# Shifted copies of V through DRAM: one write and four reads in place of sixteen SBUF copies

## The chip, the cores and the metric

One core of a Trainium2 chip. The metric is the device time of one execution in microseconds (us), the median of several runs. Ratios are the mean time of one kernel's fast runs over that of the other's in the same rounds, so not quite the ratio of the medians quoted beside them.

## The reference, cut to what matters

Four layers, A B A B, on x of 2048 positions by 512 features, with a residual and a layer norm around each. The change touches layer B, an attention over the 8 positions 0, 2, ... 14 back:

```python
W, dil = 8, 2                                  # 32 heads of 16 features
idx = pos[:, None] - (jnp.arange(W) * dil)[None, :]
kg = k[:, :, idx_c, :]                         # B, H, S, W, Dh
vg = v[:, :, idx_c, :]
logits = where(mask, einsum("bhsd,bhswd->bhsw", q, kg) * scale, -1e9)
o = einsum("bhsw,bhswd->bhsd", softmax(logits), vg)
```

## The kernel before

The 2048 positions are worked on in four blocks of 512. For each block the weights of the window lie with partition = 32 x (shift group) + head, and the product with V needs V in the same layout. So for each of four features `dl` there must be a row for every (shift, head): the same row of V, moved by 2 positions from one group of 32 partitions to the next. The kernel before makes these rows with four SBUF-to-SBUF DMAs per feature, sixteen a block, all on the one queue of SyncE (SP):

```python
def vrep(dl):
    if dl % 2 == 0:
        self.Vg[L, b][dl // 2] = self.big([2, NB * KVW], "Vg")
    for g in (0, 2, 1, 3):                     # KVW = 528, VGW = 2104 elements
        a = T["V"][dl:dl + 1, 0:1, 2 + 2 * g:3 + 2 * g]
        src = bass.AP(a.tensor, a.offset, [[4 * a.ap[0][0], H], [1, VGW]])   # 32 rows
        nc.sync.dma_start(out=self.Vg[L, b][dl // 2][32 * g:32 * g + 32, dl % 2, 0:VGW], in_=src)
# its consumer, on VectorE, once per feature q (4096 products per partition)
nc.vector.tensor_tensor(out=pv, in0=PT..., in1=<windows of Vg[q // 2][:, q % 2]>, op=ALU.mult)
```

The nine transposes of the normalised x (`xnT<-xn`) feed the projections. In layer A a small factor is already sent through DRAM and read back with broadcast (`Prho<-rd`), from a source of 8 x 16 rows:

```python
src = bass.AP(a.tensor, a.offset, [[2 * 16 * P, 8], [0, 16], [1, 16 * P]])
nc.sync.dma_start(out=pr[:].rearrange("p t a i -> p (t a i)"), in_=src)       # Prho<-rd
...
nc.sync.dma_start_transpose(out=self.xnT[...], in_=self.xn[...])              # xnT<-xn
```

The sequence of all steps (`_ORDER`), the buffer that each tile takes (`_SLOTS`) and the engine of each step that could run on two (`_CHOICE`) are fixed strings that a search has found. They give each engine its instructions in one fixed order.

## Time and profile before

| | |
|---|---|
| time | 333.1 us (332.5 to 334.3) |
| span of the profiled run | 329.5 us |
| busy: PE, VectorE (DVE), ScalarE (ACT) | 95%, 92%, 85% |
| VectorE's wait for the V copies | 1.2 us in all |
| DMA engines in the two B layers (93.7 to 173 and 247.8 to 313 us) | 80% and 92% busy, at 138 and 150 GB/s |

A busy share is time with an instruction under way, over the span. A wait line reads: who, waiting for whom: us in all, how often, the longest. The lines themselves are in the prediction.

### The profile page before, as it was taken

To read this page: it belongs to the slowest core of one execution; us is meant where nothing else is said; L and a number is where in the kernel's file an instruction comes from. 1 tells how busy PE (TensorE), PEld (TensorE's weight loads), DVE (VectorE), ACT (ScalarE), POOL (GpSimd) and SP (SyncE) were. 2 spreads that over 40 slices of the span, in tenths; PEclk is the share of its full clock that TensorE was granted. 3 is DMA by queue.
4 is the path that set the end of the run, shared out by engine and by line. 5 is a ranking of instruction groups with operands and counts; after the bars stand their busy time and mean duration, and the time that the engine had idled before them with its cause. 6 is when DMAs were issued, how large, how long until landed. Compare 5 with 4: busy or idle time off the path is not lost.

```text
span 329.5 us, 8061 instructions
## 1 busy us (share of the span) xinstructions
PE 311.5 (95%) x3203; PEld 149.7 (45%) x3203; DVE 302.7 (92%) x443; ACT 279.2 (85%) x634; POOL 26.9 (8%) x50
## 2 busy tenths in 40 slices
PE   8999999999999999899999999789999999997892
PEld 3645456435444454344443464543554444442330
DVE  8999994988999999899999999699999999999992
ACT  4999997999988979799999999699997887766550
POOL 4000000000040004000000000000004042400000
PEclk9999999999999999999999999999999999999998
DMA  7990000013757699994670300023359969799733
GB/s 200 313 252 6 0 2 4 2 47 92 127 141 152 143 156 138 139 157 98 114 148 4 64 3 2 4 69 90 116 72 190 133 130 147 138 150 160 161 115 120
DMA packets 37389, 35.42 MB, mean 107 GB/s; under 512 B 23008, under 2 KB 32224, under 8 KB 37344
## 3 DMA queue, kind: packets, MB, share of 16 engines
q1 hardware_dynamic: 36816, 34.81, 54.4%
q8 instruction: 27, 0.44, 0.7%
q14 instruction: 18, 0.15, 0.2%
q10 hardware_dynamic: 528, 0.02, 0.1%
HBM read 10.50 MB, written 2.36 MB: 39 GB/s over the span
## 4 chain that ended last, share of the span: by engine, by line
PE 60%; ACT 13%; DMA 12%; DVE 7%; SPq 3%; issue 2%; ACTq 0%; DVEq 0%
PE ps L893 18%; PE ps L516 9%; DMA Vg<-V 7%; PE ps L601 6%; PE ps L589 6%; PE ps L694 5%; DMA xnT<-xn 4%; PE ps L981 3%; ACT Ek L595 3%; ACT Eq L702 3%; PE ps L1045 2%; SPq L945 2%; DVE Eq L812 2%; PE ps L456 2%; ACT sqd L536 2%
## 5 line engine op out<-in xcount | busy, mean ns | idle before, releaser
L893 PE MATMUL ps<-xnT,WB 128*128 128x512 bf16 x384 | 88.4, 380 | 0.8 <-DMA xnT<-xn 0.8
L1036 DVE TENSOR_TENSOR pav<-PT,Vg 128x4096 bf16<-128x4096 bf16 (+1 forms) x34 | 71.8, 2162 | 1.9 <-DMA Vg<-V 1.2
L974 DVE TENSOR_TENSOR prod<-QT,K 128x4096 bf16<-128x4096 bf16 x32 | 72.2, 2285 | 0.5 <-ACT K L189 0.3
L893 PEld LDWEIGHTS <-WB 128*128 128x128 bf16 x384 | 42.3, 114 | 44.1 <-issue 7.6
L516 PEld LDWEIGHTS <-oT 128*128 128x128 bf16 x256 | 23.6, 98 | 33.6 <-ACT oT L189 4.3
L189 ACT CAST oT<-ps 128x512 bf16<-128x512 f32 (+1 forms) x55 | 29.5, 584 | 8.1 <-PE ps L1045 7.7
L702 ACT ACTIVATE Eq<-ps 128x512 bf16<-128x512 f32 x64 | 34.6, 617 | 1.3 <-PE ps L694 1.3
L595 ACT ACTIVATE Ek<-ps 128x512 bf16<-128x512 f32 x64 | 33.8, 612 | 0.8 <-PE ps L589 0.8
L516 PE MATMUL ps<-WoB,oT 128*128 128x512 bf16 x128 | 32.8, 380 | 0.3 <-ACT oT L189 0.2
L516 PE MATMUL ps<-WoA,oT 128*128 128x512 bf16 x128 | 30.9, 380 | 0.8 <-DVE oT L187 0.8
L694 PE MATMUL ps<-xnT,WA 128*128 128x512 bf16 x128 | 31.3, 380 | 0.2 <-DVE Eq L812 0.2
L536 ACT ACTIVATE sqd<-x 128x512 bf16<-128x512 bf16 x48 | 29.9, 629 | 1.3 <-DVE x L529 1.1
L601 PE MATMUL ps<-WA,xnT 128*128 128x512 bf16 x128 | 30.6, 379 | 0.0
L589 PE MATMUL ps<-WA,xnT 128*128 128x512 bf16 x128 | 30.4, 379 | 0.0
L529 DVE SCALAR_TENSOR_TENSOR x<-ps,x 128x512 bf16<-128x512 f32 x38 | 24.9, 684 | 1.4 <-PE ps L516 1.3
L189 ACT CAST K<-ps 128x512 bf16<-128x512 f32 x32 | 18.7, 591 | 3.6 <-PE ps L893 3.3
L189 ACT CAST QT<-ps 128x512 bf16<-128x512 f32 x31 | 18.2, 600 | 3.0 <-PE ps L893 3.0
L1045 PE MATMUL ps<-pav,indAV 128*32 128x512 bf16 (+1 forms) x272 | 17.5, 370 | 3.3 <-DVE pav L1036 2.9
L935 POOL COPY vh<-V 128x64 bf16<-128x64 bf16 x6 | 7.5, 1244 | 161.7 <-ACT V L189 161.7
L526 ACT ACTIVATE x<-ps 128x512 bf16<-128x512 f32 x26 | 15.1, 593 | 6.2 <-PE ps L519 5.7
L601 PEld LDWEIGHTS <-xnT 128*128 128x128 bf16 x128 | 12.3, 98 | 14.7 <-issue 0.4
L589 PEld LDWEIGHTS <-xnT 128*128 128x128 bf16 x128 | 12.3, 98 | 14.6 <-ACT xnT L189 0.4
(127 smaller groups left out, 451.1 us busy)
## 6 DMA issues: line engine op xcount, KB each, us to landing
Vg<-V SPq DMA_DIRECT2D x128, 131.5 KB, 4.5
Prho<-rd SPq DMA_DIRECT2D x8, 512.0 KB
x<-in_A_x_dram SPq DMA_DIRECT2D x3, 512.0 KB, 7.2
WB<-in_B_wqkv_dram SPq DMA_DIRECT2D x3, 512.0 KB, 8.9
wraw<-in_A_wqkv_dram SPq DMA_DIRECT2D x4, 256.0 KB, 4.5
out_dram<-x SPq DMA_DIRECT2D x4, 256.0 KB, 2.2
out_dram<-x SPq DMA_DIRECT2D x8, 128.0 KB, 2.5
x<-in_A_x_dram SPq DMA_DIRECT2D x4, 128.0 KB
```

What stands on the lines that cost most here:

```text
L189: self.nc.scalar.copy(out=out, in_=in_)
L516: nc.tensor.matmul(y[:], lhsT=oT[:, c, t * P:(t + 1) * P], rhs=Wo()[:, c, :], start=(c == 0), stop=(c == NB - 1 and not onpe))
L529: nc.vector.scalar_tensor_tensor(out=xb[:, t, :], in0=T[t][:], scalar=1.0, in1=xb[:, t, :], op0=ALU.mult, op1=ALU.add, **kw)
L536: nc.scalar.activation(out=sqd[:], in_=xb[:, t, :], func=ACT.Square, accum_out=T["ss"][:, t:t + 1])
L589: nc.tensor.matmul(pk[:], lhsT=xnT[:, t, k, :], rhs=self.WA[:, k, D:2 * D], start=(k == 0), stop=(k == NB - 1))
L595: nc.scalar.activation(out=T["E"][:, t, s, :], in_=T["k", t][:], func=ACT.Exp, scale=1.0 - 2.0 * s)
L601: nc.tensor.matmul(pv[:], lhsT=xnT[:, t, k, :], rhs=self.WA[:, k, 2 * D:3 * D], start=(k == 0), stop=(k == NB - 1))
L694: nc.tensor.matmul(pq[:], lhsT=self.WA[:, k, hb * P:(hb + 1) * P], rhs=xnT[:, :, k, :], start=(k == 0), stop=(k == NB - 1))
L702: nc.scalar.activation(out=self.Eq[L, b][s][:, :, hb, :], in_=T[hb][:].rearrange("p (t i) -> p t i", t=4), func=ACT.Exp, scale=1.0 - 2.0 * s)
L893: nc.tensor.matmul(pp[:], lhsT=self.WB[:, k, i * D + c:(i + 1) * D:NB], rhs=xnT[:, :, k, :], start=(k == 0), stop=(k == NB - 1))
L974: nc.vector.tensor_tensor(out=pr[:], in0=QT[:, c:c + 1, :].to_broadcast([P, NW, TB]), in1=win, op=ALU.mult)
L1036: nc.vector.tensor_tensor(out=pv, in0=PT[:, :, lo:lo + n].unsqueeze(1).to_broadcast([P, NB, 2, n]), in1=vw, op=ALU.mult)
```

## The change

Its intent: to move V out of SBUF once and to let one DMA per feature fetch all four shifted copies, five DMAs a block instead of sixteen. A new search made new strings for order, slots and choices. The diff, cut to its core (the strings and two options that are switched off are left out):

```diff
+    "v_dram": ((0, 0), (0, 1), (0, 2), (0, 3), (1, 0), (1, 1), (1, 2), (1, 3)),
...
+        def vwr():
+            self.VD[L, b] = self.dram.tile([P, NB * KVW], BF16, name="vd%d%d" % (L, b))
+            nc.sync.dma_start(out=self.VD[L, b][:], in_=T["V"][:].rearrange("p c t -> p (c t)"))
+
         def vrep(dl):
...
+            if (L, b) in _OPT["v_dram"]:
+                a = self.VD[L, b][dl:dl + 1, 2:3]
+                src = bass.AP(a.tensor, a.offset, [[2, 4], [4 * NB * KVW, H], [1, VGW]])
+                nc.sync.dma_start(out=self.Vg[L, b][dl // 2][:, dl % 2, 0:VGW], in_=src)
+                return
...
+        if (L, b) in _OPT["v_dram"]:
+            add(st + "v", "SP", vwr)
```

More of the change, by code (lines that the diff above doesn't have):

```diff
@@ L44 @@
     "split": ((1, 2), (1, 3)),
+    "v_dram": ((0, 0), (0, 1), (0, 2), (0, 3), (1, 0), (1, 1), (1, 2), (1, 3)),
+    "half_mo": (),
+    "rho_pad": 0,
     "warm": 14,
@@ L54 @@
 _ORDER = """
-9 d6 b6 8 e a c 0 0 d i i i 0 0 i i i f h i i i i i i i i g j k o p j l 3 1x 1y t 3 1x t u m b o q r 34 1z s t
-x 2 2 1q 1r 1x 1x 1x n 1q 21 20 1x v w w 1s 1q 22 23 1q 1q 1t 1u 1q 4i 1w y 3d 3d 3d 3e 1v 3e 4 z 6 3e z 25 z
-z 10 1h 3e z 11 25 25 25 15 13 1h 1h 5 12 12 12 16 12 26 1h 26 26 26 26 1i 3e 1 28 28 26 14 18 26 26 d5 2g 2g
-bh 2j 17 2g 18 3e 2g 18 18 19 2a 1h 1n 1j 1o 2h 2h 2h 2h 2h 2h 2h 18 1f 1a 1c 2h 1k 3d 3e 3e 1b 1b 1l 1k 1e 2k
-1k 1k 1p 1b 1b 2d 1m 2j 2j 2m 2d 7 2l 32 32 33 1d 33 2d 2d 2e 3d 2r 7 2r 1g 28 2o 2o 2d 33 2i 29 2o 2o 33 3a
@@ L60 @@
-28 2s 2s 2c 2p 3a 3a 2r 3a 35 35 35 2s 2s 2s 2s 2r 2s 32 27 2s 2j 2o 32 2b 3b 37 38 33 33 33 33 2u 2u 2u 2z 2z
-2u 3a 2z 2z 3e 30 3a 3a 2f 2f 2f 2f 2q 2q 2v 2q 2n 2q 3f 2y 35 3f 3a 3a 2z 2t 31 bs 2w 31 2x 3b 36 31 39 31 3c
-3g 3a 3c 3g 3g 3c 3c 3m 3f 3n 3o 3o 3o 3g 3g 3g 3f 3p 3q 3g 3g 3f 3r 5l 3q 24 24 24 3h 3g 3p 3t 3v 3i 3i 3u 5m
-5n 3s 3q 3q 3q 3q 3h 3i 5m 7 3p 3w 3y 3h 3h 24 24 3x 3q 3z 3q 3q 3q 3i 5l 3i 3i 3i 3i 3h 5p 5o 5m 5m 3j 5q 5m
-5r 3i 3k 5l 5s 5t 5v 5m 3k 3j 3k 5u 3k 5m 5m 7g 7h 7i 40 43 41 44 7h 42 5m 3j 3j 5m 24 7 45 3k 3k 3k 3k 24 46
@@ L65 @@
-45 47 5w 5z 5y 5x 48 60 45 49 47 45 4a 47 47 61 61 62 4b 3j 47 4b 4f 94 4c 4d 7j 61 3k 45 45 4e 45 4g 45 64 7j
-7j 4h 65 61 66 95 63 63 63 63 4k 4u 4u 67 4k 4k 4u 4v 96 63 95 97 4l 67 6a 6b 4j 4w 4m 7h 4x 7h 4p 4q 7k 7l 4k
-7n 68 4n 4p 4r 69 97 3l 6c 7m 7o 7p 50 4p 4s 50 7q 4p 7p 4t 7s 7r 7r 7p 7t 7r 7p 97 7u 4u 4y 4o 7r 4z 6j 6k 6o
-6p av 6o 6q 6o 6o 50 6t 7v 7r 6e 95 7v 6e 7y 7z 7w 95 6f 7x 6s 6r 6g 6v 6j 6l 98 99 9c 9a 6e 6v 6e 6i 4j 6d 9b
-6j 6m 9d 9d 9e 6h 6v 6j 9d 9d 9g 9f 6u 6w 6w 6w 6n 80 8c 3l 82 9f 9h 9f 9i 9f 8h 6v 6w 9j 8d 51 9f 6u 6u 6x 50
@@ L70 @@
-87 6d 6x 6w 9j 83 87 9k 6u 88 51 8j 51 51 9m 9l 6x 6v 6y 9n 9o 89 82 84 82 4z 4z 52 52 8c 8e 8c 8c 4z 85 8f 87
-87 8b 8a 8g a0 50 51 a1 a0 a0 81 52 6z 6y 6z a3 71 70 6y 6y 6z 72 6z 73 9q a2 81 9p 9r 74 75 76 8i 74 50 77 74
-78 76 76 9v 9w 74 79 76 9v 9v 53 9y 53 53 53 54 54 54 54 55 56 8i 7a 57 58 8j 82 76 7a 7d 7e 59 7c 59 8i 59 59
-7b 86 5a 5c 5b 8j 8j 5e 5b 5d 5b 5b 9x 5f 5b 7f a5 a7 5f 5j 5h 5i 9q 9s 9q 9t 5g 9q 8k 8k 8k 8k 9v a7 8l a7 8l
-a0 9u a4 8k 8l 8i c3 c3 c4 c4 c4 9z 8j b4 b5 b5 c4 c3 c4 c4 c3 c4 c4 b7 b7 b4 b5 5k b8 a8 a8 a7 a8 a8 a9 a9 b5
@@ L75 @@
-8m 8m b9 c1 8m c2 c2 a6 a6 at au a8 a9 b4 aw at at au au au au aw 8n ax 8n 8p 8n 8m 8n b5 c3 8r 8o a6 ay a7 c1
-c2 a6 au c2 8q 8s 8s 8v 8t c4 8u aa aa 8s 8s 8u 8w 8x aa 8u 8u 8y aa c1 c2 aw aw b0 8u 8y 91 b5 at 92 8z b4 b5
-b5 ab c2 ac az ab ab ae ab 90 93 ad bc bc bc bc b7 b7 af ag ah ag ag ag aj ak bb al au c1 bi au bi bf bf bf b1
-bd ai ai ai ai bi bj am ai b1 am b1 b1 aq ao an ba ar bc bg bg bg bg bg bg ag ag bf ag bl ag ap bq b2 as bq bq
-bq bg b1 bg br br br br br br b3 b3 b3 b3 be be be be c2 by by by by c2 c1 bz br br bn by bn bn c2 bt bu c5 c6
@@ L80 @@
-c6 c5 bt bn bo c5 by by by by bv c5 bn bt bi bm c6 c6 c6 c6 c6 c6 bt bk bp bp bp bz by bp c0 c0 bw bx c0 c0 c9
-c5 ca c6 cb cb cb cc cd fr ce cd c7 c8 c8 cc ch cf fs ft cg ci cc cj cm cd cl cd e2 fs e3 c7 e4 cd c7 c7 c8 c8
-c8 cd cd ck cd e3 c8 c8 c8 cd cd e2 e5 e7 c7 c8 e6 e3 e3 e3 cn co cp hb e8 cq cr hc e2 eb ea e9 fu fu ec cs ct
-e3 cu e3 e3 e3 cs cv e3 cs fs hd hc ed ee eg cs ef cw eh ei ei ei ei cx ej cu cu cu fu cy fs fv cu cy cz em d0
-d2 d3 fw fz el fx cs cs he cs cs fy g0 g0 g0 g1 d1 d4 en ek g3 ek ek ek eo ek g2 g2 g4 g2 he he dc dc eo er g0
@@ L85 @@
-g5 g2 hc dh de dh g6 g2 dj g6 g9 ga g7 di g8 d7 d7 dd d8 d7 d7 d9 hc hf hg ep hh dh dh es hj db eq dl hi dc dc
-dn dn dk d6 hk hk gb hk et ev da dm ev df f0 hl hm dg fa ew dn hn dn hm dm ho ex f1 ev ey hm fc f0 hk f2 fc hp
-hm hq do do do do f0 f0 dp dp dn f3 dm dm fc f4 do dp dn hm hq gd hr f5 f5 f5 f5 ev ht hu dq dq dq hs hv gi f7
-f6 eu f9 gi gk f8 gi fb dr dq dr dt gl ez fc gi eu gc gd gm fd gf fd fd ge gj i2 i3 dr dr fd gd gd fe fe fd fb
-gn dv gn gg fb fb gn gn gs gu gu gu fe fc go gh gp i7 i7 ds i8 i9 gv gq gv gr gt gu gv gv gw hx gw gv gw i7 ia
@@ L90 @@
-hy i7 ff fg fh ff fg gu fi ff i2 ib i4 i2 i2 hx hx i5 hx hz i6 i0 du dw dx gt ic ie if ie ie i1 dw dy gc hw id
-id id id if fg if ie if ig ig ff dw e0 fj if ig dw e1 gx gt gy fg gz fk fl fl fl fn fm fo fp fl fq ie ih ii ih
-ih ih ih ii ii ij ik gt il io ii im io gx gx gx io ii in ip iq ip is ir ip it io ir ip gy h0 gy gx h1 h4 ir gy
-dz iu ir iv dz h4 h2 h5 h5 h6 iw h8 gy iv h4 h3 h5 h4 h5 h7 h7 h9 fo ha h7 h7
+34 0 0 0 27 d5 8 i i i i i i i i i i i i i i 9 0 a d 3 4i f g c 1x h e j k 3 1x o p j l m b t t 1y av o 2 2 1q
@@ new lines @@
+1z 1x 1x u q 1r t v 21 w n 1q x r w 20 1x 1x bh 23 2i 22 1s s 1q 1q 1q 1q 1w y 3d 3e 4 3d z z z z 1u 7 7 3d 3d
+1v 1t bs 25 3e 5 18 18 18 3e 3e 10 18 z 13 15 3e 11 25 3e 1 3e 3e 19 28 16 28 28 26 28 26 29 2a 12 12 12 18 1a
+25 1e 25 1b 1c 26 26 2c 26 26 1f 2b 26 6 26 14 2g 2h 2h 1h 1h 1h 1b 1h 1d 1i 12 2g 2h 2h 1b 1b 1g 17 2j 1h 1j
+1o 2j 2l 2k 2g 2h 2h 1k 1l 1k 1n 1k 1k 2g 2r 2h 2h 2d 2d 1m 32 7 7 2d 2d 2o 2s 2s 2o 2e 2o 2o 33 33 2d 2u 24
+32 33 33 3a 2u 2w 2r 2s 1p 2s 2r 2t 2r 2s 2j 2p 3a 3a 2j 2s 2s 2s 32 2m 32 35 33 33 2o 3a 33 33 3b 2z 2z 2z 3f
@@ new lines @@
+3g 3g 2f 2f 2n 2f 2z 2f 2q 2q 36 3a 30 3d 3a 3a 3a 2u 2u 2x 2y 3f 2z 35 35 35 2q 3a 24 24 24 24 24 2q 37 2v 31
+31 3e 38 31 3g 3b 3a 31 3c 3c 3c 39 3c 3m 3f 3l 3n 3o 3o 3o 3f 3p 3q 3g 3g 3g 3g 3g 5l 3f 3h 3r 3q 3g 3p 5m 3v
+3u 3s 3i 3t 3i 3q 3q 3h 3p 3y 3w 5n 3q 3q 3h 3h 24 3z 3i 3i 3i 3i 5m 3i 3q 3x 3q 3q 3j 3k 5l 5o 5p 3i 3q 3h 3k
+3i 7g 5m 5m 5q 5m 5r 40 44 43 3j 7h 41 7i 5l 5u 5m 5s 5m 5t 7h 7j 7j 7j 3j 3k 3j 42 45 45 5v 5m 3k 3k 3k 3k 3k
+5m 5m 5w 5y 46 48 5z 45 45 5x 47 60 47 49 47 4a 47 4b 47 61 61 64 4b 4c 3j 4d 3k 94 4f 61 4g 45 45 62 45 45 4h
@@ new lines @@
+4e 61 63 63 95 96 65 4k 66 63 63 95 97 97 4u 4l 4v 67 63 4j 4p 4q 4p 4p 4p 7h 67 6a 4s 4u 68 69 6b 6c 7h 7k 7l
+7m 4r 97 7n 4k 4k 7o 4n 7p 7p 4t 4w 50 7q 4u 4u 7p 7s 4m 7p 50 b6 7t 7r 7u 6j 6j 4y 6e 6e 4x 4z 50 4z 4z 7r 7r
+7r 6k 4k 6l 7v 7r 6o 6o 6f 6e 95 95 7v 7z 7y 6g 4o 6p 7w 7x 6t 6h 4j 6q 98 9c 99 50 6v 6o 6o 6e 9a 9b 9d 6s 9d
+6j 6j 9e 9g 6r 9d 9d 6i 80 82 9f 9f 6n 51 51 6m 9h 6v 6v 9f 9i 9f 83 6d 6d 6v 51 51 52 52 9j 9f 6w 6w 6w 6w 6x
+6u 6u 50 87 6x 51 9j 9l 9m 6w 87 6x 9k 89 87 8c 8a 88 8c 9n 8e 87 6u 8h 8b 8j 6u 8c 6u 3l 6v 6y 6y 6y 6y 52 82
@@ new lines @@
+82 50 85 82 86 6z 6z 8f 71 70 9o 8c 8g 9q 9q 4z 4z 8d 6z 6z 9r 72 9s a0 73 74 a1 74 84 75 76 77 76 53 a0 53 a2
+74 81 81 74 a5 78 76 79 9q 9t 76 9v 9w 54 54 55 53 53 8i 8i 54 54 57 8i 8i 8i a0 a0 7a 76 56 a7 7a 58 59 a3 7b
+7e a4 9p a6 7d 59 5c 5a 5b 59 7c 8j 8j 5b 59 5e 8j 5d 5b 9v 9v 5b 9v 5f 9z 9x a7 9y 5b 5f 8k 5j 8k 8k 8k 8l 8l
+7f c3 c4 c4 5g c3 c3 c4 c4 c4 c4 5i b4 b5 9q 9u a6 a6 5h a7 a7 8k 8l 5k 8j b4 b4 b4 a8 a8 a8 a8 b5 b5 b5 b5 b5
+b5 a6 a9 a9 c1 c1 c1 a8 b7 a6 b7 c1 8m 8m c2 8m 8m c2 c2 c2 c2 b5 at at b8 b9 c2 c2 8n 8n 8n a9 8o a7 8n 8p au
@@ new lines @@
+au at 8r au 8q 8s au 8s 8t aa aa au au bc aa 8s 8v 8s 8w 8u 8x 8u 8u 8u aw ax at au b7 aw ba aw 8y 8u ay ab ab
+ac ad ab aa ab af 8y 91 c3 ae ag 90 au 8z 92 bc b7 ag c4 bc bc c4 bd bb b1 ag ah aj ak c2 ai ag ai al ai b1 ai
+am 93 aw bf bf bf b1 b0 b1 ai am ar aq bg bg bi an ag ao bg bg bg ag ag bc bg az bj ap b2 ag as b1 bf bg bi bg
+bn bk bi bq bq bq br br br br by by by by br br bq br bl bz br bn b3 b3 b3 b3 be bn be be be bt bt bt bu bv bn
+by by bo by bw by by c5 bn c6 c6 c5 c6 c6 bi bm bz bt c5 c6 c6 c5 c6 c6 bp bp bp bp c0 c0 by c0 bx c0 c1 c9 ca
@@ new lines @@
+cb cb c5 c2 c6 cc c7 cb cd ce c3 c4 cd fr fs cc cg c8 c8 e2 cf cd cd ch cd ft fs cc cl ci cd cj c7 c7 c8 e3 c8
+c8 ck c8 cd c7 e4 c8 c8 cd cd cm cd cn e3 cp co cr cq e2 e5 e3 hb e7 e6 e3 e3 c7 c8 cs e2 ea fu fu fu hc e8 e3
+e9 e3 e3 ct eb e3 ec cs cs hd e3 hc cs cx he cv cu ed ef eg he ee he eh cw ei fs cu ei cu cu ei ei el ej cy cu
+fs fv em cy d0 cz fw fx d2 cs cs cs d3 cs fy fz g0 d4 ek en d1 g1 ek ek ek eo g0 g0 g4 g0 ek eo es d7 ep eq g3
+g2 g2 g2 er g5 g2 dh d7 d8 g6 hc hc dc dd dc de di d7 da g2 d9 dn dh dc dj df g6 ga hf d6 hg g7 hj et dh dh dk
@@ new lines @@
+ev ev g8 g9 hi ex hh d7 db dc dg f0 fa dn dn dn hk hk dl d6 eu gb f1 hk ew ho f0 f2 hn hl hm hm dm dm hm f0 f3
+f0 f4 fc hk hp ev ey fc fc do hm do dm do dm do dp dp ev dn ez hq fc gi gj do dp hm gd ge fd fd fd dn fd hq hu
+hs f5 f5 f5 f5 dm ht hr hv gn fe fe gd gi f9 f6 f8 f7 gf go gi gl dq dr ds dq dr dq gs dr i2 fd dt dq gu gk gu
+gd du fb i3 fb fb fb fe i2 i4 gg dr dv gv fc gn gp gd gh gu gn gq gn i7 i7 eu gc gr gc hw i9 hx hy gi gm ic i8
+ff ff i7 ia i2 i5 i7 ib hx hz fg gu fh fg fi gv gv gv gt gw fb ie gt gt hx i0 ie hx i1 i2 ie i6 ie dw dw dx id
@@ L94 @@
+dy id id if if if if id id gw ig gv ff ff ig dw e0 if ig ie fg dw fg fj fk fl fm fl fl fl gw fp ih fn gt e1 ih
+fq fo fo dz dz ii ii ih ii ih ij gu ih gt il gx gx gx gx ik ii im io ip iq ir io ip is ir ii in io ip it ir io
+ip iu ir gy gz iv gy h0 gx gy h1 h4 gy h2 h4 h5 h6 h7 h5 iw iv gy h8 h4 h3 h5 h4 h7 h9 h7 h5 ha h7
 """
 _CHOICE = (
-    "0010111111000111110111100110000010000011111000000100011101111110010000100111000000001000000000111111"
-    "1010101100100000110010000000000000001111010001010000010100000000000000101100111100000100110000000000"
@@ L100 @@
-    "0000000000001101110000000000110100011001101101011001111000000000000000000111111001010010000101111000"
-    "00000000000001111100100001011000000000000000000000000010010000000000000000000001111"
+    "0101111111111111110111111010000010000000000000000011011011111100000000110101000001001000000011101111"
+    "1111111100110000001000000000000000001111110000010000101100001000000000101111111100000011001000000000"
+    "0000000000001101110010000010010001011100111001011001111111000000000000000111111101101100001101110000"
@@ L102 @@
+    "00000000000001111000100001001000000000000000000000000000110000000000000000000001111"
 )
@@ L106 @@
     "big": (
-        "0123456701320130457324713267153206153201453724037524160375412546307154307524375027605476"
+        "0123456701234560123451203471520365201320437204572104365721046571304625736214576217064270"
     ),
     "med": (
-        "0123456789abcdef37428c74c46c4632c5d7ab8637ba632c26a8325dc53c269ba2b7db5c763b2ab9d9a27d982178bf4a635c"
-        "87fbd94a352168c7efd0"
+        "0123456789abcdef38569a389a89811ca0156df39853f6dcafd98c3014569c8df613596d104c8f34c58fd3c7fa8d4be510a9"
+        "68d43c51be7fa08296d3"
     ),
     "t2": (
-        "0123450123425103245013245103245103245103245013520415203415230421354213054213054230154032145012354012"
-        "3540123540125340215024"
+        "0123450123412054231054210354210354210354210425013450132450123415024150324153024135041325014253014253"
+        "0142530142531042315301"
     ),
     "ps": (
-        "0123456701243576102435671043756142375641263741502317514237164572304651270346512703462751023467514361"
-        "5704263075142637042165730416573021576302145760231450736124507326147326504176235016723450167245016247"
-        "0531647253104672504136274027463124706345016243517624310624136024153024153074216530742126531072465371"
-        "4263507614230671542017540312675302146702437165042316507423165024103126037561237615246137526147532641"
-        "7035426710354627103564270"
+        "0123456701234605137256041372504673510642731506273506427306254061354027165304721653014762537071632475"
+        "1063274506132750432617054234705361427503614275063714205637412056374105674256147235164702351647032516"
+        "7403125674032516703254701647021546702146024156203415620317456231704623170642531704256317034215674301"
+        "2536407125630172456307245316027456032174532046531274605312746053127540613754206173506175063175063417"
+        "5062347502317465032741650"
     ),
@@ L302, in setup @@
         self.RD = {}
+        self.VD = {}
         self.constants()
@@ L812, in mulp @@
             nc.vector.tensor_tensor(out=ev, in0=src[:].rearrange("p (a i) -> p a i", a=NB), in1=ev, op=ALU.mult)
+        pitch = (16 + _OPT["rho_pad"]) * P
         def wr():
-            self.RD[L, b] = rd = self.dram.tile([8, 2, 16, P], BF16, name="rd%d%d" % (L, b))
-            a = rd[0:1, 0, 0:1, :]
-            dst = bass.AP(a.tensor, a.offset, [[P, 16], [2 * 16 * P, 8], [16 * P, 2], [1, P]])
+            self.RD[L, b] = rd = self.dram.tile([8, 2, pitch], BF16, name="rd%d%d" % (L, b))
+            a = rd[0:1, 0, 0:P]
+            dst = bass.AP(a.tensor, a.offset, [[P, 16], [2 * pitch, 8], [pitch, 2], [1, P]])
             nc.sync.dma_start(out=dst, in_=T["rho"][:])
@@ L822, in rdb @@
             T["P", s] = pr = self.med([4, NB, P], "Prho")
-            a = rd[0:1, s, 0:1, :]
-            src = bass.AP(a.tensor, a.offset, [[2 * 16 * P, 8], [0, 16], [1, 16 * P]])
+            a = rd[0:1, s, 0:P]
+            src = bass.AP(a.tensor, a.offset, [[2 * pitch, 8], [0, 16], [1, 16 * P]])
             nc.sync.dma_start(out=pr[:].rearrange("p t a i -> p (t a i)"), in_=src)
@@ L848, in s_a3, with bc2 @@
             return
+        def bc2(pr):
+            for t in (2 * pr, 2 * pr + 1):
+                for s in range(2):
+                    if t == 0:
+                        T["pb", s] = {}
+                    T["pb", s][t] = self.ps()
+            for hb in range(NB):
+                for s in range(2):
+                    for t in (2 * pr, 2 * pr + 1):
+                        nc.tensor.matmul(T["pb", s][t][:, hb * P:(hb + 1) * P],
+                                         lhsT=self.indB[32 * t:32 * t + 32, hb, :, :],
+                                         rhs=T["rho"][32 * t:32 * t + 32, s, :], start=True, stop=True,
+                                         tile_position=(32 * t, 0))
+        if (L, b) in _OPT["half_mo"]:
+            for pr in range(2):
+                add(st, "PE", bc2, pr)
+                for t in (2 * pr, 2 * pr + 1):
+                    for s in range(2):
+                        direct = _CHOICE[self.nflex] == "1"
+                        self.flex(st, bev, s, t)
+                        add(st, "DVE", mulp, s, t, direct)
+            return
         for s in range(2):
@@ L860, in s_a4, with mo @@
         T = {}
-        def mo():
+        def mo(k, m):
+            w = TB // m
             for r in range(4):
-                T[r] = self.ps()
+                if k == 0:
+                    T[r] = self.ps()
             for s in range(2):
@@ L868, in mo, with ev @@
                     for r in range(4):
-                        nc.tensor.matmul(T[r][32 * hb:32 * hb + 32, :],
+                        nc.tensor.matmul(T[r][32 * hb:32 * hb + 32, k * w:(k + 1) * w],
                                          lhsT=self.R[32 * r:32 * r + 32, self.reg(s, hb), :],
-                                         rhs=self.Eq[L, b][s][32 * r:32 * r + 32, :, hb, :],
+                                         rhs=self.Eq[L, b][s][32 * r:32 * r + 32, k * 4 // m:(k + 1) * 4 // m, hb, :],
                                          start=(s == 0), stop=(s == 1), tile_position=(32 * r, 32 * hb))
-        def ev(r, dve):
+        def ev(r, k, m, dve):
             if (key, b) not in self.oT:
                 self.oT[key, b] = self.med([NB, TB], "oT")
-            self.copy(dve, self.oT[key, b][:, r, :], T[r][:])
-        add(st, "PE", mo)
-        for r in range(4):
-            self.flex(st, ev, r)
+            w = TB // m
+            self.copy(dve, self.oT[key, b][:, r, k * w:(k + 1) * w], T[r][:, k * w:(k + 1) * w])
+        m = 2 if (L, b) in _OPT["half_mo"] else 1
+        for k in range(m):
+            add(st, "PE", mo, k, m)
+            for r in range(4):
+                self.flex(st, ev, r, k, m)
         self.s_out(st + "o", key, b, lambda: self.WoA, False)
@@ L941, in vrep @@
                 self.Vg[L, b][dl // 2] = self.big([2, NB * KVW], "Vg")
+            if (L, b) in _OPT["v_dram"]:
+                a = self.VD[L, b][dl:dl + 1, 2:3]
+                src = bass.AP(a.tensor, a.offset, [[2, 4], [4 * NB * KVW, H], [1, VGW]])
+                nc.sync.dma_start(out=self.Vg[L, b][dl // 2][:, dl % 2, 0:VGW], in_=src)
+                return
             for g in (0, 2, 1, 3):
```

## The prediction

- k is the number of DMA engines that one DMA uses; a "ring" is one of these engines. A "receipt" in the expectations is the time until a DMA counts as landed.
- k = 4 for the reads and 16 for the write are estimates by likeness: 8 outermost in Prho's source had a share of 0.52, 32 in the old copies 1.06. That the 4 would be the same engines each time is taken from Prho's second read, which did not raise the share.
- The sum: 93.7 + 156 + 65 + 147 + 16.5 = 478 us of span, 482 as a run, set at 455. Its 3 us for a transpose is the author's estimate (before: 2.1 us for the issue and 4.4 to landing in the median).
- The 13 us of the first rival are 8.2 for the reads and about 5 for the write until it has landed. About 2 of it had no trace behind it; the one small write in the trace of before, rd<-rho, lands after 2.3 us in all.

> **What bounds the kernel now.** I read the page first (busy times, slices), then the waits of the compute engines, then the copies by tile, then the stretches in which the two kinds of DMA that matter run alone.
>
> ```profile
> PE 311.5 (95%) x3203; PEld 149.7 (45%) x3203; DVE 302.7 (92%) x443; ACT 279.2 (85%) x634; POOL 26.9 (8%) x50
> ...
> DVE  8999994988999999899999999699999999999992
> ...
> DMA  7990000013757699994670300023359969799733
> GB/s 200 313 252 6 0 2 4 2 47 92 127 141 152 143 156 138 139 157 98 114 148 4 64 3 2 4 69 90 116 72 190 133 130 147 138 150 160 161 115 120
> ...
> q1 hardware_dynamic: 36816, 34.81, 54.4%
> ...
> HBM read 10.50 MB, written 2.36 MB: 39 GB/s over the span
> ```
>
> Three compute engines are packed side by side: the span of 329.5 us is only 18 us longer than PE's busy time and 26.8 us longer than VectorE's. The DMA engines are full in exactly two stretches, the two B layers, and move no more than about 150 GB/s there. Those are the V copies. Does anyone wait for them?
>
> ```profile
> DVE pav L1036 <- DMA Vg<-V: 1.2, 1, 1.2
> ```
>
> Once, for 1.2 us: the present order of instructions hides the copies, although just barely, because the DMA engines have nothing to spare there. The chain that ended last gives Vg<-V 7% and the issuing queue 2%, but that chain only followed the last release; VectorE was working meanwhile (100% busy from 290 to 320 us). So the change can gain little by itself. It can lose a lot, if the new route is slower than the old one in those two full stretches. That is what I worked out next.
>
> ```profile
> L945 SPq DMA_DIRECT2D Vg<-V x128: 467/592/2144, 93.7 to 310.5; - x128
> ...
> DMA to landing us min/median/max: 2.8/4.5/8.7
> ```
>
> ```profile
> 74.00:76.00 2.00, 2.00 (x70) 1.21 (x68) 1.26 (x8) 1.47 (x6) 0.00 (x0) 1.00 0.52 131
> 76.00:78.00 2.00, 1.99 (x22) 1.23 (x21) 1.77 (x6) 1.97 (x5) 0.00 (x0) 1.00 0.52 131
> ```
>
> ```profile
> 295.00:300.00 5.00, 3.65 (x47) 1.31 (x40) 5.00 (x3) 1.77 (x4) 0.00 (x0) 1.00 1.06 149
> ```
>
> The last two columns of a stretch are the mean busy share of the 16 DMA engines and GB/s. From 295 to 300 us only V copies run: all 16 engines busy, 149 GB/s, so 9.3 GB/s an engine, and a row of 4208 bytes (2104 bf16) takes 4208/9.3 = 452 ns. From 72 to 80 us only the two reads Prho<-rd run, 0.52 MB each, issued at 70.6 and about 71.4 us: the share stays at 0.52 for 8 us, two DMAs in flight or not. Half of the engines worked, 131/8 = 16.4 GB/s each, and the second read did not use the other half.
>
> [...] Prho's source has dimensions 8 x 16 x 2048, its destination 128 partitions: k = 8. The trace agrees (0.52, and no gain from the second DMA). The old V copies have 32 on both sides: k = 16, and the share of 1.06 agrees. [...] The 64 KB write rd<-rho lands in 2.3 us[...].
>
> **The change, part by part.**
>
> *Removed:* 128 SBUF-to-SBUF copies of 32 rows. Per block of 512 positions: 16 copies, 512 rows, 32 rows on each of 16 engines, 32 x 452 ns = 14.5 us of all engines, and 16 x 0.59 = 9.5 us of issue on SP. Over the kernel 4096 rows, 1850 engine-us of the 2870 (54.4% of 16 x 329.5) that the queue used.
>
> *Added, the write:* per block 128 rows of 4224 bytes, contiguous in DRAM, k = 16: 8 rows an engine, 2.1 to 3.6 us at 257 to 452 ns a row[...].
>
> *Added, the reads:* per block 4, one per feature, each 128 rows of 4208 bytes. The source pattern is 4 x 32 x 2104: four shifts outermost. The destination has 128 partitions. So k = 4, and as with Prho all four reads use the same[...] engines. At Prho's 16.4 GB/s a row takes 257 ns (a row there is 4096 bytes, about the same). One read is 32 rows an engine, 8.2 us; the four of a block queue up to 32.9 us; the 16 reads of a layer to 131.6 us, against 58 us of copies before. The row got almost twice as fast, but the engines became four.
>
> *Moved:* the order, the buffer slots and the choice VectorE/ScalarE were searched anew. Counting the two strings by kind of step: VectorE gets 5 more residual adds, 6 more direct multiplies, 1 more normalisation, 5 more evictions of transposed x and 2 of K, and gives up 3 evictions of layer A's v, 4 of its o and one of a weight: with the durations of the page (684 for a residual plus 82 for its accumulator, 680, 686 ns and so on) +4.6 us on VectorE, -8.6 on ScalarE, -1.2 on PE (five identity matmuls of 230 ns). That would be worth a few us either way. The block order stays the same in kind: transposes of the normalised x stand between V reads on the one SP queue, so they wait behind up to four reads on the four slow rings.
>
> *The sum.* The stretches of before, from the SP queue's timeline: start to the first V copy 93.7 us; V copies of the first B layer until about 173 (last issue near 171, plus landing); 75 us until the first V copy of the second B layer at 247.8; V copies until about 313; 16.5 us to the end. In the changed kernel the two V stretches, 79 and 65 us, are replaced by what four rings need: reads 131.6, four writes of about 3 us, and transposes of 3 us each in between (four in the first layer, one in the second): 156 and 147 us. The 75 us between shrink to perhaps 65, since compute has run ahead as far as its in-order queues allow. 93.7 + 156 + 65 + 147 + 16.5 = 478 us of span; the median run lies 3.9 above the profiled span, 482. This takes the four rings as never idle, which is a lower bound for that rate, and the rate as Prho's, which is the pessimistic one of those seen (see the second rival). I set 455.
>
> **Rivals.**
> - *All 16 engines are used after all* (the pattern is lowered in another way). Then a block's reads are 8.2 us at 16 x 16.4 = 262 GB/s, with the write some 13 us instead of 18.4 (the last V eviction ended at 289.3, the last copy landed at 307.7 us). No one waited for V longer than 1.2 us, so only the new order can gain: VectorE at 302.7 + 4.6 plus the 16 us of idle time that the start, the end and the two turns from A to B cost in any order gives 323 at best; about 331 us as a run. Against it: Prho is built in just this way and got 8.
> - *Four engines, but faster rows.* From 8 to 12 us the plain loads moved 356 GB/s at a share of 1.06, 21 GB/s an engine, so 200 ns a row: 25.7 us a block, 103 a layer, and the sum becomes 422, as a run 425. If rows went at 26 GB/s, 82 us a layer, 380. [...] Against it: Prho had the same long rows and only eight engines, and got 16.4.
> - *The reads are hidden* because VectorE is the bound anyway: its work in a B layer fits in the 65 to 79 us of before, and the reads need 103 to 131. They cannot be hidden, whatever the order.
> - *Buffers make it worse:* a read waits for the slot of an earlier Vg, product or pav, all in one pool of 8, while those wait for reads; the four rings then idle. Up to 20 us more, above 500.
>
> **Range and chances.** The rate of a row sets it: 26 GB/s gives 380, 21 gives 425, 16.4 gives 482, with buffer waits 505. 80% between 385 and 510, centre 455. About 1 in 10 that the engine count is not 4 in the changed kernel; then it is within 2%, or a little faster if the new order is good. Faster 0.04, same 0.08, slower 0.88.
>
> **What would show it.** In the changed profile: HBM read 10.5 + 17.2 = 27.7 MB, written 2.4 + 4.3 = 6.7 MB; 32 issues Vg<-vd of 526 KB, landing 8 us after issue when alone and up to 30 when queued; in the B layers a DMA share near 0.25 to 0.3 at 65 to 85 GB/s; VectorE's wait for DMA Vg rising from 1.2 us to about 100, PE and VectorE busy near 65 to 70%, their busy times within 5 us of before. A share near 1 with 250 GB/s or more in the B layers, or reads landing within 4 us, would prove the engine count wrong, and with it the prediction.

## The result, and the profile after

416.3 us (415.1 to 418.0) against 333.1: slower, ratio 1.250 with a 95% interval of 1.244 to 1.255.

From the page of the changed kernel: busy times, the slices of the DMA engines and of what they moved, the queue and the memory traffic.

```profile
PE 326.9 (79%) x3181; PEld 153.2 (37%) x3208; DVE 301.8 (73%) x433; ACT 281.9 (68%) x638; POOL 21.2 (5%) x50
...
DMA  8940001389419421939313000234429433213431
GB/s 228 292 95 0 3 3 33 84 164 95 155 47 114 150 100 60 153 116 95 99 59 43 11 2 5 78 103 89 107 91 114 129 140 143 106 61 123 161 129 58
...
q1 hardware_dynamic: 36048, 39.13, 44.3%
...
HBM read 27.74 MB, written 6.68 MB: 83 GB/s over the span
```

VectorE and ScalarE do the same work as before, within 1% (301.8 against 302.7 us, 281.9 against 279.2). The span grew by 85 us, so all of that is waiting. The DMA engines are no longer nearly full in the B layers: where the slices mostly said 5 to 9 tenths they now mostly say 1 to 4. The 9s that are left fall on stretches in which a transpose is under way, and there the share is no measure of work (from 170 to 172 us it reads 6.54). The engines wait for DMAs that leave most DMA engines idle. The memory traffic is what the prediction worked out (27.7 and 6.7 MB).

The changed kernel in a stretch in which only V reads run. The last two columns are the share of 16 DMA engines and GB/s:

```profile
305.00:310.00 5.00, 5.00 (x48) 2.26 (x46) 4.95 (x8) 4.66 (x12) 0.00 (x0) 1.00 0.25 103
```

A share of 0.25 is read as four engines of 16 (halves and k8 below have 0.13 and 0.54). They move 103/4 = 26 GB/s each, so a row of 4208 bytes takes 162 ns, and the 16 reads of a layer (8.6 MB) take 84 us.

Who waits, from the list of waits of the changed kernel; the last line is SP, the queue that issues the DMAs:

```profile
DVE pav L1081 <- DMA Vg<-vd: 50.1, 15, 14.5
...
PEld L698 <- DMA xnT<-xn: 20.8, 2, 16.8
PE ps L698 <- DMA xnT<-xn: 19.9, 2, 16.3
PEld L927 <- DMA xnT<-xn: 19.6, 4, 8.6
...
PE ps L927 <- DMA xnT<-xn: 16.4, 3, 8.2
```

```profile
SPq L983 <- DMA vd<-V: 53.1, 8, 15.1
```

VectorE's wait for V rose from 1.2 to 50.1 us. PE and its weight loads (PEld, the same wait seen twice) now wait for transposes too. Those were not changed. The author's guess was that they need the engines that the reads fill; that is not shown as such, but split16, k8 and tr_act below show what their time goes with. The transposes by tile, before and after (duration of the issue on SP in ns: shortest, median, longest):

```profile
L447 SPq DMA_TRANSPOSE xnT<-xn x9: 1717/2117/4264, 85.1 to 265.2; - x9
```

```profile
L451 SPq DMA_TRANSPOSE xnT<-xn x9: 1737/11172/15220, 85.0 to 311.9; - x9
```

Even the issue of a transpose took 11.2 us in the median instead of 2.1, and held SP for that long. The writes of V were late as well: one issued at 348.6 us landed 15.6 us later, where a write took 3.0 us in the median when the reads used all 16 engines (one16). The chain that ended last, before (its line by engine) and after:

```profile
PE 60%; ACT 13%; DMA 12%; DVE 7%; SPq 3%; issue 2%; ACTq 0%; DVEq 0%
```

```profile
DMA 30%; PE 26%; DVE 4%; SPq 4%; ACT 3%; issue 2%; DVEq 0%
DMA xnT<-xn 15%; DMA Vg<-vd 11%; PE ps L927 7%; PE ps L520 5%; DMA vd<-V 4%; PE ps L605 3%; PE ps L593 3%; SPq L544 2%; PE ps L698 2%; PE ps L1090 2%; DVE pav L1081 1%; SPq L451 1%; ACT oT L192 1%; PE ps L668 1%; DVE Eq L816 1%
```

The chain reaches back to 125.9 us. DMAs are 30% of the span in it, 124 us, where the whole chain of before had 12% (40 us). The transposes are the largest part, ahead of the reads themselves. A smaller effect on top: PE's granted clock was 0.90 in the mean (0.995 before), because it fell to 0.5 in PE's long waits: in the one before 186 us PE stopped at 169.5 us, the clock went to 0.5 at about 173 us, and it was back at 1.0 from 190 us, 4 us after PE had work again. PE's busy time is 15 us longer for nearly the same work (313.2 us in split16, which has the same order and a clock of 0.99).

By stretches, from the issues on SP and the rates: first read at 96.7 us; reads of the first B layer until 213; then 85 us until the first read of the second, at 298.4; reads until 402.6; 11.6 us to the end. Before, the same stretches were 93.7, 79, 75, 65 and 16.5 us.

### The profile page after: what moved, and what is told of

The parts are those of the page before. It is cut to its first block, busy times and chain, and to the rows that moved or that the text cites. A ratio compares the mean times of both kernels' runs of the same rounds, so it can differ in the third digit from the quotient of the medians.

```text
span 414.2 us, 7890 instructions
## 1 busy us (share of the span) xinstructions
PE 326.9 (79%) x3181; PEld 153.2 (37%) x3208; DVE 301.8 (73%) x433; ACT 281.9 (68%) x638; POOL 21.2 (5%) x50
## 4 chain that ended last, share of the span: by engine, by line
DMA 30%; PE 26%; DVE 4%; SPq 4%; ACT 3%; issue 2%; DVEq 0%
DMA xnT<-xn 15%; DMA Vg<-vd 11%; PE ps L927 7%; PE ps L520 5%; DMA vd<-V 4%; PE ps L605 3%; PE ps L593 3%; SPq L544 2%; PE ps L698 2%; PE ps L1090 2%; DVE pav L1081 1%; SPq L451 1%; ACT oT L192 1%; PE ps L668 1%; DVE Eq L816 1%
## 5 line engine op out<-in xcount | busy, mean ns | idle before, releaser
L1081 DVE TENSOR_TENSOR pav<-PT,Vg 128x4096 bf16<-128x4096 bf16 (+1 forms) x34 | 72.9, 2166 | 53.7 <-DMA Vg<-vd 50.1
L927 PE MATMUL ps<-xnT,WB 128*128 128x512 bf16 x384 | 92.5, 395 | 17.5 <-DMA xnT<-xn 16.4
L192 ACT CAST oT<-ps 128x512 bf16<-128x512 f32 (+1 forms) x59 | 31.6, 579 | 41.6 <-PE ps L1090 39.0
L698 PE MATMUL ps<-xnT,WA 128*128 128x512 bf16 x128 | 34.0, 412 | 20.2 <-DMA xnT<-xn 19.9
L1090 PE MATMUL ps<-pav,indAV 128*32 128x512 bf16 (+1 forms) x272 | 21.0, 420 | 33.8 <-DVE pav L1081 33.0
L520 PE MATMUL ps<-WoB,oT 128*128 128x512 bf16 x121 | 34.5, 407 | 1.0 <-issue 0.5
L192 ACT CAST QT<-ps 128x512 bf16<-128x512 f32 x31 | 18.2, 591 | 16.5 <-issue 9.0
L698 PEld LDWEIGHTS <-WA 128*128 128x128 bf16 x128 | 12.5, 104 | 37.3 <-DMA xnT<-xn 20.8
L533 DVE SCALAR_TENSOR_TENSOR x<-ps,x 128x512 bf16<-128x512 f32 x33 | 22.1, 686 | 2.9 <-PE ps L520 2.9
L530 ACT ACTIVATE x<-ps 128x512 bf16<-128x512 f32 x31 | 18.3, 606 | 8.3 <-PE ps L523 8.3
L1090 PEld LDWEIGHTS <-indAV 128*32 128x32 bf16 x272 | 5.6, 99 | 48.1 <-DVE pav L1081 36.9
L192 ACT CAST V<-ps 128x512 bf16<-128x512 f32 x31 | 17.6, 596 | 3.9 <-PE ps L927 3.9
```

The costliest lines, as they stand in the source:

```text
L192: self.nc.scalar.copy(out=out, in_=in_)
L520: nc.tensor.matmul(y[:], lhsT=oT[:, c, t * P:(t + 1) * P], rhs=Wo()[:, c, :], start=(c == 0), stop=(c == NB - 1 and not onpe))
L698: nc.tensor.matmul(pq[:], lhsT=self.WA[:, k, hb * P:(hb + 1) * P], rhs=xnT[:, :, k, :], start=(k == 0), stop=(k == NB - 1))
L927: nc.tensor.matmul(pp[:], lhsT=self.WB[:, k, i * D + c:(i + 1) * D:NB], rhs=xnT[:, :, k, :], start=(k == 0), stop=(k == NB - 1))
L1081: nc.vector.tensor_tensor(out=pv, in0=PT[:, :, lo:lo + n].unsqueeze(1).to_broadcast([P, NB, 2, n]), in1=vw, op=ALU.mult)
L1090: nc.tensor.matmul(po[32 * c:32 * c + 32, lo:lo + n], lhsT=self.indAV[:], rhs=T["p", q][:, c, hf, lo:lo + n], start=(hf == 0), stop=(hf == ...
```

## The experiments

The theory: the outermost size 4 of the new source pattern leaves each read on four of 16 engines, the same four for all reads. Rival 1: the round trip through DRAM is what costs. Rival 2: the new order is bad in itself. A kernel with the new order and the old SBUF copies would have been the plain test of rival 2. It could not be run: the new slots give V's buffer away as soon as V is written to DRAM, and with the old copies the build ends in a deadlock.

The rates in the table are those of one stretch each; other stretches of a run give other rates. "Same" below means within 2% of before.

| run | what | engines for a V read | GB/s while reading | time, us |
|---|---|---|---|---|
| before | SBUF copies of 32 rows | 16 | 149 | 333.1 |
| after | one read per feature | 4 | 103 | 416.3 |
| halves | two reads per feature | 2 | 52 | 582.8, one run |
| k8 | wrong rows, 8 outermost | 8 | 125 | 374.8, one run |
| split16 | sixteen reads of 32 rows | 16 | 253 | 334.2 |
| pair8 | eight reads of 64 rows | 16 | about 230 | 335.5 |
| one16 | wrong rows, one read per feature | 16 | 381 | 333.7 |
| before_pair8 | old order, route of pair8 | 16 | about 240 | 337.5 |

**split16: the same route, cut so that 32 is outermost.**

```diff
-                src = bass.AP(a.tensor, a.offset, [[2, 4], [4 * NB * KVW, H], [1, VGW]])
-                nc.sync.dma_start(out=self.Vg[L, b][dl // 2][:, dl % 2, 0:VGW], in_=src)
+                for g in (0, 2, 1, 3):
+                    a = self.VD[L, b][dl:dl + 1, 2 + 2 * g:3 + 2 * g]
+                    src = bass.AP(a.tensor, a.offset, [[4 * NB * KVW, H], [1, VGW]])
+                    nc.sync.dma_start(out=self.Vg[L, b][dl // 2][32 * g:32 * g + 32, dl % 2, 0:VGW], in_=src)
```

Expected:

> Each read of the changed kernel cut into four, one per shift, so that 32 rows are outermost on both sides; still from DRAM, same order, same buffers. Theory (the outermost size of 4 leaves each read on four engines): 16 engines work, the DMA share in the B layers is near 1 while reads run instead of 0.25, VectorE's wait for Vg falls from 50 us to under 6, and the time to 326 to 338 us. Rival 1 (the round trip through DRAM, write and then read, is what costs): the wait for Vg stays above 30 us and the time above 380. Rival 2 (the new order is bad in itself): the wait goes, the time stays above 380.

Measured: correct, 334.2 us (333.4 to 336.6), ratio to before 1.005 (1.000 to 1.0095): the same. The wait of the product for Vg is gone from the list. A stretch with reads of split16 only:

```profile
134.00:140.00 6.00, 6.00 (x52) 2.73 (x51) 5.86 (x8) 5.94 (x16) 0.00 (x0) 1.00 1.01 253
```

All 16 engines work. Same order, same buffers, same DRAM tile, same bytes, four times as many DMAs, and 82 us of the 83 are back. Both rivals fall.

**pair8: eight reads a block.** For a fixed shift the two features of a tile become an inner dimension:

```diff
+                if dl % 2 == 0:
+                    for g in (0, 2, 1, 3):
+                        a = self.VD[L, b][dl:dl + 1, 2 + 2 * g:3 + 2 * g]
+                        src = bass.AP(a.tensor, a.offset, [[4 * NB * KVW, H], [NB * KVW, 2], [1, VGW]])
+                        nc.sync.dma_start(out=self.Vg[L, b][dl // 2][32 * g:32 * g + 32, :, 0:VGW], in_=src)
```

> Eight reads a block: one per shift and pair of features, 32 rows outermost, two features inside, 64 rows each. Theory: as with the cut into sixteen, 16 engines, but half of the issues on SP (0.6 us each): 324 to 336 us, not slower than split16. Rival 1 and 2: above 380, as there.

Measured: correct, 335.5 us (334.4 to 336.7), ratio 1.008 (1.004 to 1.012): the same, and in the range. Half of the issues gained nothing over split16, so there is no sign that SP's issue time held that back. A wait of 1.1 us for Vg came back; a pair lands 5.6 us after its issue in the median, a single one 3.1.

**halves: two engines.**

```diff
+                for g in (0, 2):
+                    a = self.VD[L, b][dl:dl + 1, 2 + 2 * g:3 + 2 * g]
+                    src = bass.AP(a.tensor, a.offset, [[2, 2], [4 * NB * KVW, H], [1, VGW]])
+                    nc.sync.dma_start(out=self.Vg[L, b][dl // 2][32 * g:32 * g + 64, dl % 2, 0:VGW], in_=src)
```

> Each read cut into two halves of 64 partitions, with 2 shifts outermost: only the number of engines should change, the wrong way. Theory: two engines, DMA share 0.125 and 51 GB/s while only reads run; a block's 512 rows need 256 x 162 ns = 41.5 us, a layer 166 us instead of 83; the time rises by about 2 x 83 to 540 to 600 us. If something else than the outermost size limits the reads (issue, receipt, DRAM): 410 to 430 us.

Measured: correct, 582.8 us in one run. A stretch with reads only, in which no compute engine has anything to do:

```profile
112.00:120.00 8.00, 0.00 (x0) 0.00 (x0) 0.00 (x0) 0.00 (x0) 0.00 (x0) 0.50 0.13 52
```

Two engines of 16 at 26 GB/s each. The time rose by 166.5 us over that of after, where 2 x 83 = 166 was expected. So close a match is partly luck, in one run and with other waits rising too (PE's for transposes from 37.4 to 89.2 us). With split16 it says that the number of engines is the cause; k8 and one16 below add eight engines and a single read on 16.

**bcast: why a row took 162 ns and not 257.**

```diff
-                src = bass.AP(a.tensor, a.offset, [[2, 4], [4 * NB * KVW, H], [1, VGW]])
+                src = bass.AP(a.tensor, a.offset, [[2, 4], [0, H], [1, VGW]])
-    "rho_pad": 0,
+    "rho_pad": 8,
```

> Wrong result on purpose, to find why a row took 162 ns and not the 257 ns that I took from the Prho reads: the 32 rows of each shift are now read from one and the same DRAM row (step 0), as Prho does, and Prho's own row pitch in DRAM is widened from 4 to 6 KB. Theory A (re-reading one DRAM row is slow): V reads fall from 103 to about 66 GB/s, 257 ns a row, and the time rises to 470 to 510 us; Prho stays at 131 GB/s. Theory B (the 4 KB pitch is slow): Prho rises towards 8 x 26 = 208 GB/s, V reads stay at 103 GB/s, the time at 410 to 420. Theory C (eight engines get less each than four): neither moves.

Measured: 419.6 us in one run, wrong. From 104 to 108 us the V reads had 102 GB/s at a share of 0.25; from 72 to 76 us Prho had 138 GB/s at 0.54. Neither moved as its theory asked (V reads 103 before, Prho 131):

```profile
104.00:108.00 4.00, 4.00 (x20) 1.78 (x17) 3.84 (x6) 3.42 (x9) 0.88 (x1) 1.00 0.25 102
```

```profile
72.00:76.00 4.00, 4.00 (x79) 2.17 (x78) 3.12 (x12) 3.71 (x13) 0.00 (x0) 1.00 0.54 138
```

Re-reading one row and the pitch are out, and theory C was left, to be tried in k8 and one16.

**before_pair8: the route without the new order.** The kernel of before, with the write and the eight reads of pair8 in the place of its copies, nothing else:

```diff
+            if dl == 0:
+                self.VD[L, b] = self.dram.tile([P, NB * KVW], BF16, name="vd%d%d" % (L, b))
+                nc.sync.dma_start(out=self.VD[L, b][:], in_=T["V"][:].rearrange("p c t -> p (c t)"))
+            if dl % 2 == 0:
+                for g in (0, 2, 1, 3):   # as in pair8
```

> The kernel of before with its own order, slots and choices; only the route of V is new: one write of V to DRAM ahead of the first copy, then eight reads a block with 32 rows outermost. It tells the route from the new order. If the route on 16 engines is as good as the SBUF copies: 329 to 336 us, wait of pav for Vg at most 3 us. If the faster reads (about 250 GB/s instead of 149) free something that the order can use: below 329. If the write's receipt ahead of the reads hurts an order that was made without it: 337 to 350.

Measured: correct, 337.5 us (337.0 to 338.2), ratio 1.014 (1.010 to 1.018): the same by the 2% rule, but the interval lies above 1, and it is the third case of the expectation at its lower edge. The product never waits for Vg. But SP waits 25.7 us for the writes to land before it may issue the reads, transposes stand behind it in the same queue, and PE waits 6.3 us for them. The new order, made for this route, comes to 335.5 us with it (pair8); the intervals of the two ratios overlap, so a gain from the new order is not shown.

**k8: eight engines.** Wrong rows, same bytes.

```diff
-                src = bass.AP(a.tensor, a.offset, [[2, 4], [4 * NB * KVW, H], [1, VGW]])
+                src = bass.AP(a.tensor, a.offset, [[1, 8], [4 * NB * KVW, 16], [1, VGW]])
```

> Wrong result on purpose: the reads of the changed kernel with 8 outermost instead of 4 (wrong rows, same bytes, same row length, same destination). A row took 162 ns on two and on four engines and 257 on eight in the Prho reads. If the number of engines sets that: V reads at a share of 0.5 and 131 GB/s, 66 us a layer, time 350 to 375. If it belongs to Prho's pattern: 205 GB/s at 0.5, 41 us a layer, time 333 to 350.

Measured: 374.8 us in one run. A stretch with four reads:

```profile
116.00:120.00 4.00, 4.00 (x20) 2.10 (x19) 3.86 (x4) 3.97 (x8) 0.00 (x0) 1.00 0.54 125
```

Eight engines at 125/(0.54 x 16) = 14.5 GB/s each: mostly the rate of Prho, as the first case said (in some stretches of the second B layer it went up to 185 GB/s, 21 GB/s an engine). In this stretch twice the engines brought only a fifth more. That seemed to say that the number of engines sets the rate of one. one16 shows that it does not.

**pool: the reads issued from GpSimd.** Only `nc.sync` became `nc.gpsimd` in the read.

The first case is that the reads then spread over all 16 engines.

> The four reads of a block as they are (4 shifts outermost), but issued from GpSimd instead of SP. [...] four reads in flight use all 16 engines: DMA share near 1 while reads run, wait for Vg below 10 us, transposes on SP no longer behind them in the same queue, time 333 to 350[...]. If all four stay on the same engines: share 0.25, time 390 to 425.

Measured: correct, 378.3 us in one run, between the two cases, so it settles little. The share rose above 0.25 as soon as four reads were out (0.85 from 118 to 120 us, 0.60 to 122), which agrees with reads spread over more engines:

```profile
118.00:120.00 2.00, 2.00 (x13) 0.99 (x10) 1.30 (x4) 1.97 (x7) 0.72 (x2) 1.00 0.85 91
120.00:122.00 2.00, 2.00 (x11) 1.03 (x10) 2.00 (x1) 1.97 (x5) 0.00 (x0) 1.00 0.60 164
```

But GpSimd's reads wait too: 35.7 us for the writes to land, and 81 us for buffers (32.6, 31.3 and 17.0), and its own small copies of V's edge come behind that (one at 140.2 us, after a wait of 20.2).

**tr_act: the transposes issued from ScalarE.** Only `nc.sync` became `nc.scalar` in the transpose.

> The changed kernel with the nine transposes of x issued from ScalarE's queue instead of SP's; the V reads stay on four engines. It splits the loss of 83 us into the reads themselves and the transposes that stand behind them in SP's queue. If the first-in first-out order behind the reads is what delays the transposes (37 us of waits for xnT, 11 us of SP time for each issue): waits for xnT fall below 12 us, SP is free, time 375 to 400. If the transposes are slow because the four engines are busy, whatever the queue: 405 to 425.

Measured: correct, 452.1 us in one run, slower than either case, so both were wrong about the time. The waits for xnT did not fall but rose, from 37.4 to 56.3 us, and the issue of a transpose, at 5.0 us in the median, took less than half of the 11.2 of after, but still up to 11.5:

```profile
L451 ACTq DMA_TRANSPOSE xnT<-xn x9: 1716/4976/11544, 86.3 to 346.1; - x9
```

PE's longest wait for a transpose was 18.7 us, against 16.3 in after. So it is not the place behind the reads in SP's queue alone that makes them slow. What they go with is the number of engines that the reads use: on SP the median issue took 11.2 us with four read engines, 6.4 with eight (k8), but 2.5 and 1.9 with all 16 (split16, one16); with two (halves) PE waited 89.2 us for transposes, against 37.4 with four. Moved to ScalarE, they hold up an engine that has other work: SP then waits 93 us for ScalarE's evictions of V.

**one16: what the change was meant to be.** One read per feature, the same bytes, from 128 evenly spaced rows. The rows are wrong.

```diff
-                src = bass.AP(a.tensor, a.offset, [[2, 4], [4 * NB * KVW, H], [1, VGW]])
+                src = bass.AP(a.tensor, a.offset, [[NB * KVW - 64, 128], [1, VGW]])
```

> Wrong result on purpose: the four reads of a block as in the changed kernel, one DMA per feature, the same bytes and row length, but from 128 evenly spaced rows (one dimension of 128 instead of 4 x 32), so that nothing but the outermost size differs. It is what the change was meant to be, if its addresses allowed it. Theory: 16 engines, share near 1 and 240 to 270 GB/s (16 GB/s an engine, as on eight), a read of 0.54 MB in about 2.2 us plus its receipt; wait of pav for Vg under 3 us; time 328 to 335, since VectorE and PE are as busy as before. If it comes out below 327, the intent was good for more than the two cuts (334 and 336 us) show, and what those lost is in their issues.

Measured: 333.7 us (332.6 to 335.5), ratio 1.004 (0.998 to 1.010), the same: the time is in the range, the rate was not. With reads only:

```profile
132.00:136.00 4.00, 4.00 (x26) 1.82 (x27) 4.00 (x3) 3.97 (x12) 0.00 (x0) 1.00 1.00 381
```

16 engines at 24 GB/s each. So theory C is wrong: an engine of 16 can get nearly what one of two or four gets. And the best route of all, 2.5 times as fast as the old copies, gains nothing: no one had waited for V.

**ports and before_ports: the destination.** Wrong rows: in split16, and in the kernel before, each DMA of 32 rows writes every fourth partition instead of 32 neighbours. The first case in each expectation is that the destination sets the rate; the labels name a cause for it that no run shows. The edit is the same in both:

```diff
-                    nc.sync.dma_start(out=self.Vg[L, b][dl // 2][32 * g:32 * g + 32, dl % 2, 0:VGW], in_=src)
+                    nc.sync.dma_start(out=self.Vg[L, b][dl // 2][g:128:4, dl % 2, 0:VGW], in_=src)
```

> Wrong result on purpose: split16 with only the destination partitions changed: each of its DMAs of 32 rows writes every fourth partition instead of 32 neighbouring ones. It asks why an engine moved 26 GB/s in reads on two and four engines and in the single reads on 16 (one16), but only 16 in split16, k8 and Prho. [...] GB/s divided by 16 x share rises from 16 to 22 or more while reads run. If small DMAs of two rows an engine are what is slow: it stays at 16 to 17. The time stays at 331 to 337 in both.

> Wrong result on purpose: the kernel before with the destination of each SBUF copy changed in the same way, to every fourth partition. [...] they go from 9.3 GB/s an engine (149 in all) to 13 or more; if the reading from SBUF limits them, they stay at 9 to 10. Time 328 to 336 in both.

Measured: 339.1 and 330.3 us, one run each. First ports, then before_ports, in stretches with V traffic only:

```profile
114.00:120.00 6.00, 6.00 (x30) 3.07 (x29) 5.70 (x5) 5.97 (x14) 0.00 (x0) 1.00 0.74 214
```

```profile
272.00:278.00 6.00, 6.00 (x46) 3.01 (x39) 5.87 (x4) 5.09 (x13) 0.82 (x2) 1.00 0.56 218
```

From DRAM the rate of an engine is 214/(0.74 x 16) = 18 GB/s, less than the 22 that I had asked for. It is hardly a rise: split16 itself had between 253/(1.01 x 16) = 15.7 and 243/(0.85 x 16) = 17.9 in different stretches. Between SBUF and SBUF it went from 9.3 to 218/(0.56 x 16) = 24.3 GB/s. The old copies were slow because of where they wrote: nothing but the destination partitions differs between the two. Why the destination matters is not shown. For reads from DRAM the destination alone does not explain 16 (split16) against 24 (one16), as ports had 18; that stays open. The layout that the product needs does not allow the faster destination: one shift belongs to 32 neighbours.

**quad: the intent, made correct.** V is written four times with row pitch 2120, each time moved by its shift, so that partition p finds its row at an even spacing.

```diff
-            nc.sync.dma_start(out=self.VD[L, b][:], in_=T["V"][:].rearrange("p c t -> p (c t)"))
+            w = NB * KVW + 8
...
+            for g in range(4):
+                a = self.VD[L, b][g * P:g * P + 1, 8 - 2 * g:9 - 2 * g]
+                dst = bass.AP(a.tensor, a.offset, [[w, P], [1, NB * KVW]])
+                nc.sync.dma_start(out=dst, in_=T["V"][:].rearrange("p c t -> p (c t)"))
...
+                a = self.VD[L, b][dl:dl + 1, 10:11]
+                src = bass.AP(a.tensor, a.offset, [[4 * (NB * KVW + 8), P], [1, VGW]])
```

> A correct kernel with one read per feature on 16 engines: V is written four times, each copy moved by its shift, so that the rows for the 128 partitions lie evenly spaced in DRAM; four writes and four reads a block instead of one and four. If the even spacing is all that the change lacked: reads at 340 GB/s or more as in one16, no wait of pav for Vg, 331 to 338 us, level with the kernel before. If the three more writes (1.6 MB a block) and their receipt are felt: 338 to 350.

Measured: correct, 349.0 us (344.0 to 349.5). Two of four runs are counted as slow, since they are over 1.5% above the fastest. The fast ones give a ratio of 1.044 (1.035 to 1.053), slower: the second case of the expectation. The profile is of a run counted as slow (349.5 us), so its numbers are rough: the reads do run at about 400 GB/s on 16 engines, but the writes land 5.7 us after issue in the median instead of 3.0 (one16), and SP waits 41.9 us for them instead of 21.0. VectorE waits 8.9 us for Vg.

No correct version here beats the kernel before.

## Why the prediction was right, and which steps were off

The direction, the size (range 385 to 510, measured 416) and the mechanism were right. That the number fell into the range was partly luck: the rate of a row decided it, and with the rate that was measured, 26 GB/s, the prediction's own sum gives 380, just outside the range. Other terms that were too short, above all the stretch between the two B layers, brought it back in. By its steps:

- *The change can gain little by itself.* Right, and shown: one16 has the ideal route and comes to 1.004 of before.
- *k = 4, all reads on the same engines.* Right: share 0.25, and halves and k8 follow the outermost size to 0.13 and 0.54. Prho's 0.52 with 8 outermost had pointed to it before the change was ever run.
- *A row takes 257 ns.* Mis-sized: 162 ns. This is the main reason why 455 was too long: the reads of a layer took 84 us and not 131.6. Prho's rate held for the eight engines of k8 and not for four. Why was narrowed (not the repeated row, not the pitch, not the number of engines as such) but not settled. The second rival in the prediction had this rate in it, as an assumption.
- *Rows at 26 GB/s give 380.* This row of the sum was too short by some 34 us. Its terms were: first stretch 106 us, between 65, second 97, end 16.5. Measured: 117, 85, 104 and 11.6.
- *The 75 us between the layers shrink to 65, since compute has run ahead.* Wrong: they grew to 85. Compute had not run ahead. PE waits in order for transposes, once for 16.3 us just before 186 us, and so layer A's matmuls, which do not need V, were late too.
- *Transposes cost 3 us each on the four engines.* Mis-sized: their issue alone held SP for 11.2 us in the median, and PE waited 37.4 us for them. They are the largest item of the chain. tr_act shows that another queue did not help (56.3 us of waits); split16 and one16, that they are fast again (issue 2.5 and 1.9 us, no wait of PE or PEld over 1.5 us) when the reads use all engines.
- *VectorE's wait for Vg about 100 us.* It was 50.1, in line with the faster row. VectorE also waited once for 17.9 us, until 192.9 us, for QT from ScalarE; ScalarE had waited 16.8 us for PE, and PE 16.3 us for a transpose. A full split of the 83 us was not made. PE and VectorE were busy 79% and 73% of the span, where 65 to 70% was expected.
- *The choices move +4.6 us to VectorE and −8.6 from ScalarE.* Wrong by a misreading: in the residual step a "1" means PE and ScalarE, not VectorE. With that sign VectorE loses 3.1 us and ScalarE 0.7. The busy times differ by −0.9 and +2.7 us. PE adds five identity matmuls (31 against 26) and does not lose five. Either way it is nothing beside 83 us.
- *Memory traffic 27.7 and 6.7 MB; busy times within 5 us.* Right for the traffic, VectorE and ScalarE. PE's rose by 15 us, from the lower clock, which the prediction did not think of.
- *Smaller readings.* The two stretches of before called full were 80% and 92% busy. The last copy of V did not land at 307.7 us: four more were issued from 308.7 us on, and landed by about 313. The 3.9 us between the median run and the span mixes two runs; within the profiled run it is 1.8.
